# Whole matmuls for the first heads' values, and a last query group in two halves

## The chip, the cores and the metric

The kernel runs on one NeuronCore of a Trainium2 chip. Its engines work side by side and meet only at semaphores: TensorE (PE; its weight loads are the row PEld), VectorE (DVE), ScalarE (ACT), GpSimd (POOL) and SyncE (SP), which issues most DMAs. The metric is device time in microseconds (us) of one execution. The kernel before takes 806.93 us, the median of three executions (806.62, 806.93, 809.84).

## The reference

`x` is 2048 x 640 in bf16. Two attention layers with 32 heads of 20 columns read it, and a gate mixes them:

```python
g = sigmoid((x * gate_w).sum(-1))          # one number per token
qkv = x @ wqkv                             # A and B have weights of their own
# A: every query against all 2048 keys
o_a = softmax(q @ k.T * 20**-0.5) @ v
# B: every query against 8 keys, 0, 2, ... 14 tokens back
o_b = softmax(<q, k[s - 2*w]> * 20**-0.5, w = 0..7) @ v[s - 2*w]
out = g * (o_a @ A_wo) + (1 - g) * (o_b @ B_wo)
```

A is nearly all of the work: 32 x 2048 x 2048 exponentials.

## The kernel before, in words

**Units, tiles and rides.** A's work is cut into 32 groups (`GROUPS`): 512 queries (`qc`, 0 to 3) of four heads (`q`, 0 to 7; `q` 0 holds heads 0 to 3). A group has 64 *units*, one for each of 16 blocks of 128 keys (`kb`) and each of the four heads (`j`). A unit is a 128 x 512 block of scores. `qk` (line 1659) makes two or three units at a time into a PSUM tile `score0` or `score1`, one matmul per unit, the four heads on four 32-row strips of the array. `exp` (L1682) turns the tile into weights in one of five `ebuf` buffers, on ACT. `pv` (L1723) multiplies them with the values `vA` into the PSUM tile `obank`, the heads on four column strips. A unit can instead *ride*: its scores go to a spare bank and DVE makes the exponential with integer arithmetic (L1672, then three shifted copies by L879, each multiplied with values that POOL has scaled into `vS`, L870).

**Order of the work.** `_Sched` records each instruction with a cost in the source. The main loop goes tile by tile: `qk`, `exp`, a `pv` slot, then `spend`, which fills PE with side work (projections, layer B, output products, and filler matmuls of no use to the result, L1744) until a limit after the end of the exponential before. Side work is a set of generators (`gen_...`) with priorities. The table `PLAN` changes the loop's parameters at given tile numbers: the limits (`SLACK`), the conditions for a ride (`DWAIT`, `DIDLE`, `DTIME`, ...), the fillers (`FILL`) and the priorities. Its last entry is for tile 700. All of this runs on the host; what reaches the chip is a fixed list of instructions per engine.

**Start.** The inputs are loaded, `x` is turned on PE, keys and queries of group 0 are made, then `v_first` (L1387 to 1393) makes the values of heads 0 to 3 for key blocks 0 to 3, and `gen_v(0)` (L779) those of blocks 4 to 15 in two banks of six. One block is five accumulating matmuls (the contraction is 640) of 80 columns, and each of these is issued as four matmuls on 32-column strips of the array, with a weight load each: 16 x 5 x 4 = 320 pairs of weight load and matmul. `gen_q1` then makes the queries of group 1.

**Group ends and the kernel's end.** When a group's last `pv` is issued, `close` starts `gen_norm` (L817): DVE transposes `obank` (L819) and takes reciprocals of the sums (L823), POOL (in the last group DVE) scales by them and by the gate (L829, L837), DVE transposes back (L853) and DMAs store the result in `oTd`. For the last group `tail` (L1147) follows: `gen_prefold` has put part of the output product of the last 512 tokens into SBUF (`pre`), `gen_prefold2` another part into two PSUM banks; `tail` adds the rest on PE (L1156), adds up on DVE and ACT (L1173, L1179, L1182) and stores four blocks of 128 tokens (L1187).

Of the kernel before, what the change touches and what calls it, by code (L numbers as in the profile page):

```python
# [14 lines left out]
P = 128  # L15
# [21 lines left out]
VP = lambda q: 0 if q == 0 else 1 if q < 4 else 2  # L37

# [293 lines left out]
def _build(ctx, nc, A_x, A_wqkv, A_wo, B_wqkv, B_wo, gate_w, out):  # L332
# [446 lines left out]
    def gen_v(part):  # L779
        m = (6, 2, 1)[part]  # L780
        for kb in range(4 if part == 0 else 0, KBN, m):
            while part == 2 and g1 < 2 + VPACE * kb / KBN:
                yield ("cond",)
# [610 lines left out]
    def v_out():  # L1394
        return v_copy(0, 0, 4, 0)
# [524 lines left out]
```

## Time and profile before

| | |
|---|---|
| median of three executions | 806.93 us |
| the profiled execution | 807.63 us, its span from first to last instruction 805.8 us |
| mean granted TensorE clock | 0.992 |
| ACT: all busy, and the exponentials alone | 777.7 us, 765.2 us in 727 tiles |
| DVE, PE, POOL busy | 713.9, 759.5, 140.3 us |
| first exponential starts, last exponential ends | 19.35 us, 797.61 us |

Busy time is a share of the span; a busy PE counts matmuls that overlap each other, fillers among them. "issue" in the column of waits is time in which an engine waited for no semaphore that the profile shows. A row of the timeline begins with its start and its length in microseconds.

### The profile page before, as it was taken

The numbers are of one execution on the slowest core, as the hardware profiler recorded it, in microseconds if no ns is written. First come the engines' busy times: TensorE is split into PE (matmuls) and PEld (weight loads), VectorE is DVE, ScalarE is ACT, GpSimd is POOL, SyncE is SP. The second block draws the span as 40 slices with busy tenths as digits, with TensorE's granted clock in tenths as the row PEclk, the third lists the DMA queues.
The fourth block names the chain that finished last, engine by engine and source line by source line (L and its number), as shares of the span: only waits on it lengthen the run. The fifth ranks groups of instructions, "written<-read, shape, count | busy, mean of one in ns | idle before, by whom it ended". The sixth has DMA issues, their size and how long they took to land.

```text
span 805.8 us, 29670 instructions
## 1 busy us (share of the span) xinstructions
PE 759.5 (94%) x12485; PEld 279.4 (35%) x12485; DVE 713.9 (89%) x1286; ACT 777.7 (97%) x762; POOL 140.3 (17%) x239
## 2 busy tenths in 40 slices
PE   8899989999899999999999999899999999999997
PEld 4343232322234333342344344233334333433232
DVE  6568879999989899979889989998998999898995
ACT  4599999999999999999999999999999999999996
POOL 5002411114321111011110111111011111111120
PEclk9799999999999999999999999999999999999999
DMA  9120010112011121031112013003113001303000
GB/s 300 56 46 7 20 28 19 37 32 73 14 26 36 44 55 32 13 78 24 34 48 64 13 39 77 20 21 77 25 32 69 18 23 34 80 7 70 16 7 35
DMA packets 59448, 35.27 MB, mean 44 GB/s; under 512 B 25252, under 2 KB 58116, under 8 KB 59316
## 3 DMA queue, kind: packets, MB, share of 16 engines
q1 hardware_dynamic: 59028, 33.05, 16.6%
q8 instruction: 99, 1.62, 0.8%
q10 hardware_dynamic: 288, 0.33, 0.1%
q14 instruction: 33, 0.27, 0.1%
HBM read 11.45 MB, written 2.62 MB: 17 GB/s over the span
## 4 chain that ended last, share of the span: by engine, by line
ACT 45%; PE 33%; issue 18%; DVE 2%; DMA 1%; SPq 0%; ACTq 0%; DVEq 0%
ACT ebuf L1682 44%; PE score L1659 11%; PE obank L1723 9%; PE side L591 6%; PE score L591 4%; DMA oB<-in_A_x_dram 1%; DVE uD L1672 1%; PE obank L1744 1%; PE side L967 0%; DVE uD L879 0%; PE side L1744 0%; PE score L1334 0%; PE score L1744 0%; ACT eB L998 0%; PE score L967 0%
## 5 line engine op out<-in xcount | busy, mean ns | idle before, releaser
L1682 ACT ACTIVATE ebuf<-score 128x1024 bf16<-128x1024 f32 (+1 forms) x727 | 765.2, 1237 | 11.2 <-PE score L1659 10.4
L1659 PE MATMUL score<-qT,kT 32*128 32x512 bf16 x2023 | 292.4, 385 | 32.0 <-ACT ebuf L1682 23.2
L1672 DVE TENSOR_SCALAR uD<-score 128x512 int16<-128x512 f32 x355 | 237.8, 682 | 17.7 <-PE score L1659 16.5
L879 DVE TENSOR_SCALAR uD<-uD 128x2048 int16<-128x2048 int16 x285 | 192.9, 694 | 10.6 <-PE obank L1723 9.9
L1659 PEld LDWEIGHTS score<-qT,kT 32*128 32x128 bf16 x2023 | 71.3, 91 | 278.5 <-ACT ebuf L1682 211.7
L1723 PE MATMUL obank<-ebuf,vA 128*21 128x512 bf16 x1668 | 165.3, 387 | 0.8 <-DVE uD L879 0.7
L870 POOL TENSOR_TENSOR vS<-vA,vw 128x252 bf16<-128x252 bf16 x95 | 59.9, 632 | 458.0 <-DVE uD L879 238.5
L1723 PE MATMUL obank<-uD,vS 128*21 128x512 bf16 x1140 | 100.4, 379 | 0.0
L591 PE MATMUL side<-xT,kvw 128*32 128x256 bf16 (+1 forms) x2000 | 85.6, 287 | 0.9 <-DVE oB L633 0.5
L1723 PEld LDWEIGHTS obank<-ebuf,vA 128*21 128x21 bf16 x1668 | 40.9, 89 | 99.9 <-issue 77.9
L591 PEld LDWEIGHTS side<-xT,kvw 128*32 128x32 bf16 x2000 | 47.8, 96 | 29.3 <-issue 15.4
L951 DVE TENSOR_TENSOR stage<-qkvB 128x1280 bf16<-128x1280 bf16 x64 | 51.1, 819 | 0.0
L1049 DVE TENSOR_TENSOR stage<-stage,eB 128x1280 bf16<-128x1280 bf16 x64 | 50.9, 821 | 0.0
L837 POOL TENSOR_TENSOR oN<-oTt,rcp 128x256 bf16<-128x256 f32 (+1 forms) x61 | 37.8, 632 | 46.6 <-DVE uD L879 27.2
L591 PE MATMUL score<-xT,kvw 128*32 128x256 bf16 (+2 forms) x760 | 34.8, 291 | 0.3 <-DVE uD L1672 0.3
L1723 PE MATMUL obank<-uD,vA 128*21 128x512 bf16 x380 | 34.3, 379 | 0.0
L935 DVE CAST qkvB<-side 128x512 bf16<-128x512 f32 (+1 forms) x53 | 30.7, 589 | 2.2 <-PE side L591 2.2
L1723 PEld LDWEIGHTS obank<-uD,vS 128*21 128x21 bf16 x1140 | 27.5, 91 | 9.3 <-issue 2.9
L819 DVE STREAM_TRANSPOSE oTt<-obank 128x512 f32<-128x512 f32 x32 | 22.7, 710 | 8.0 <-PE obank L1723 8.0
L591 PE MATMUL side<-kvw,xT 128*32 128x320 bf16 (+2 forms) x680 | 25.7, 283 | 2.1 <-issue 2.1
L829 POOL TENSOR_TENSOR rcp<-rcp,gA 128x16 f32<-128x16 f32 x31 | 6.9, 222 | 115.4 <-DVE rcp L823 40.5
L591 PE MATMUL side<-woBp,oB 128*32 128x128 bf16 (+1 forms) x520 | 24.6, 294 | 0.3 <-DVE oB L1074 0.2
(201 smaller groups left out, 583.1 us busy)
## 6 DMA issues: line engine op xcount, KB each, us to landing
stage<-qkvB SPq DMA_DIRECT2D x128, 82.5 KB
stage<-in_B_wqkv_dram SPq DMA_DIRECT2D x1, 2400.0 KB
oTd<-oN SPq DMA_DIRECT2D x108, 20.0 KB
WqP<-in_A_wqkv_dram SPq DMA_DIRECT2D x13, 160.0 KB
qT<-dst SPq DMA_DIRECT2D x104, 20.0 KB
out_dram<-outsb SPq DMA_DIRECT2D x12, 160.0 KB
kvw<-in_A_wqkv_dram SPq DMA_DIRECT2D x2, 800.0 KB
qT<-qbnd SPq DMA_DIRECT2D x72, 1.0 KB
```

The source lines that it names most:

```text
L591: ins = e.matmul(o[j:k, :], l(j) if callable(l) else l[:, j:k], r, start=(first and i == 0), stop=(last and i == n - 1), skip_group_check= ...
L819: T("dve", 0.623, lambda e: e.transpose(oTt[:, :], obank[:, :]), reads=["obank"], writes=["oTt"])
L837: T(en, c2 if half < 0 else 0.56, lambda e: e.tensor_tensor(oo, ii, ib, ALU.mult), reads=["rcp", "oTt"], writes=[("oN0", h) for h in ((0, ...
L870: T("pool", 0.62, lambda e: e.tensor_tensor(vS[:, d % NVS, :, :], _ap(vA, (kb * NQ + q) * 4 * DV, [[0, K - 1], [1, 4 * DV]]), _ap(vw, 0, [ ...
L879: T("dve", 0.066 + 0.1334 * n, lambda e, k=k: e.tensor_scalar(uD[u][:, 0:512 * n].bitcast(I16), uD[u][:, 0:512 * n].bitcast(I16), SHIFTS[k ...
L935: t = TB(dvc(n * TOK), lambda e, o=o, i=i: e.tensor_copy(o, i), reads=[("side", b)], writes=[key])
L951: TB(dvc(CN * TOK, 2), lambda e, w=w, ks=ks: e.tensor_tensor(prodB(w), qB[:, :, :], ks, ALU.mult), reads=["qB", "kB"], writes=[("prod", w) ...
L1049: TB(dvc(CN * TOK, 2), lambda e, o=o, vs=vs, ee=ee: e.tensor_tensor(o, vs, ee, ALU.mult), reads=["eB", ("prod", k)], writes=[("prod", k + ...
L1659: ins = e.matmul(o, kT[32 * j:32 * j + 32, q, kb * P:(kb + 1) * P], qT[g % NQT][32 * j:32 * j + 32, :], start=True, stop=True)
L1672: t = T("dve", 0.6, lambda e: e.tensor_scalar(uD[d % NU][:, 512 * i:512 * (i + 1)].bitcast(I16), side[y], UOFF, 0.0, op0=ALU.add, op1=ALU. ...
L1682: exps[s] = T("act", actc(512 * n), lambda e: e.activation(ebuf[s % NE][:, 0:512 * n], score[s % 2][:, 0:512 * n], ACTF.Exp, scale=LN2 / S ...
L1723: ins = e.matmul(obank[32 * j:32 * j + DV, :], v, src, start=(kb == 0), stop=(last and k >= len(lst) - 4), skip_group_check=True)
```

## The change

Three things change.

- **Values of heads 0 to 3.** `v_first` makes two key blocks instead of four, `gen_v(0)` the other fourteen in three banks (5, 5 and 4 blocks). Each accumulating step is one matmul over all 128 columns of the array instead of four on strips: 16 x 5 = 80 pairs. Its planned cost is 0.064 us.
- **The last group.** `GROUPS` gets its last entry twice. Both copies are `HALVED`: a unit is still 512 columns wide, but holds 256 queries of *two* key blocks, so each copy has 32 units. `qk` and `pv` issue two matmuls of 256 columns for such a unit; a riding unit needs two scaled sets of values, the second in a part of `xT` that is free by then. Each half has its own `gen_norm` on 256 columns. After the first half `gen_half` finishes and stores token blocks 0 and 1 while the second half runs; `gen_prefold` puts a fourth piece into SBUF, and `tail` is left with blocks 2 and 3.
- **Table.** `PLAN` is replaced as a whole; its last entry is for tile 740. All its parameters are other ones: `SLACK` is mostly (0.28, 0.73) where it was mostly (0.30, 0.64), and up to 0.93 at the end.

The diff, cut to its core:

```diff
+LASTQ = len(GROUPS) - 1
+GROUPS.append(GROUPS[LASTQ])
+HALVED = [False] * LASTQ + [True] * 2
+kbs = lambda g, kb: (2 * kb, 2 * kb + 1) if HALVED[g] else (kb,)
...
 def gen_v(part):
-        m = (6, 2, 1)[part]
-        for kb in range(4 if part == 0 else 0, KBN, m):
+        for kb in (2, 7, 12) if part == 0 else range(0, KBN, m):
...
-                                    mmc(VCN[part]), per=5 if part == 0 else 2 if part == 1 else 1)
+                                    mmc(VCN[part]) if part else 0.064, per=(5, 2, 1)[part], whole=part == 0)
...
 def gen_norm(g):
-        T("dve", 0.623, lambda e: e.transpose(oTt[:, :], obank[:, :]), reads=["obank"], writes=["oTt"])
+        W = 256 if HALVED[g] else 512
+        T("dve", 0.623 if W == 512 else 0.35, lambda e: e.transpose(oTt[:, 0:W], obank[:, 0:W]), reads=["obank"], writes=["oTt"])
...
+    def gen_half():
+        while not (done.get("prefold1") and done.get(("norm", LASTQ))):
+            yield ("cond",)
+        for blk in range(2):
+            b = yield from bank()
+            yield from mm_group(b, fold_mms(side[b][:, :], blk, 0, 512, 1) + fold_mms(side[b][:, :], blk, 0, 512, 2), rd, mmc(512))
+            t = T("dve", dvc(512), lambda e, b=b, blk=blk: e.tensor_tensor(tcol(blk, 0, 512), side[b][:, :], pre(blk), ALU.add), ...)
+        b = yield from bank()
+        for blk in range(2):
+            yield from mm_group(b, fold_mms(o, blk, 512, D, 1) + fold_mms(o, blk, 512, D, 2), rd, mmc(128), per=3)
+        t = T("dve", dvc(256), lambda e, b=b: e.tensor_tensor(trest(0), sap(b, 0, [[P, 2], [1, P]]), prest(0), ALU.add), ...)
+        for blk in range(2):
+            tail_out(blk, "sp")
...
 def tail():
+        T("dve", dvc(256), lambda e: e.tensor_tensor(trest(2), _ap(rest, 0, [[P, 2], [1, P]]), prest(2), ALU.add), ...)
+        T("act", actc(512), lambda e: e.activation(tcol(3, 0, 512), side[tail_bank[3]][:, :], ACTF.Copy), ...)
+        T("dve", dvc(512), lambda e: e.tensor_tensor(tcol(2, 0, 512), side[tail_bank[2]][:, :], pre(3), ALU.add), ...)
+        tail_out(2, "sp")
+        tail_out(3, "act")
...
 def v_first():
-            for kb in range(4):
+            for kb in range(2):
                 for c, (o, l, r) in enumerate(v_mms(side[0][:, 80 * kb:80 * kb + 80], kb, 0)):
-                    for j in range(0, P, 32):
-                        ins = e.matmul(o[j:j + 32, :], l[:, j:j + 32], r, start=(c == 0), stop=(c == CN - 1), skip_group_check=True)
+                    ins = e.matmul(o, l, r, start=(c == 0), stop=(c == CN - 1), skip_group_check=True)
...
 def qk(s):
+            for t in range(2):
+                for g, kb, j, o in lst:
+                    kl = kbs(g, kb)
+                    q, n, c = GROUPS[g][1], 512 // len(kl), 256 * max(0, g - LASTQ)
+                    ins = e.matmul(o[:, n * t:n * t + n], kT[32 * j:32 * j + 32, q, kl[t] * P:(kl[t] + 1) * P],
+                                   qT[min(g, LASTQ) % NQT][32 * j:32 * j + 32, c:c + n], start=True, stop=True)
```

More of the change, by code (lines that the diff above doesn't have):

```diff
@@ L425, in _build @@
     vS = sb([P, NVS, K - 1, 4 * DV], BF16, "vS")
+    vSd = lambda d, t: xT[:, 2 + d % NVS, 0:(K - 1) * 4 * DV].rearrange("p (a b) -> p a b", b=4 * DV) if t else vS[:, d % NVS, :, :]
     gtr0 = qkvB[:, S:S + 1024].bitcast(FP32)
@@ L574, in release, with mm_group @@
         bank_free[b] = t.end + LAT[t.stream]
-    def mm_group(b, mms, reads, cost, first=True, last=True, per=1):
+    def mm_group(b, mms, reads, cost, first=True, last=True, per=1, whole=False):
         n = len(mms)
@@ L588, in fn @@
                     n_ = P if callable(l) else l.shape[-1]
+                    if whole:
+                        ins = e.matmul(o, l, r, start=(first and i == 0), stop=(last and i == n - 1), skip_group_check=True)
+                        continue
                     for j in range(0, n_, 32):
@@ L780, in gen_v @@
         m = (6, 2, 1)[part]
-        for kb in range(4 if part == 0 else 0, KBN, m):
+        for kb in (2, 7, 12) if part == 0 else range(0, KBN, m):
             while part == 2 and g1 < 2 + VPACE * kb / KBN:
                 yield ("cond",)
+            m = 4 if kb == 12 and part == 0 else 5 if part == 0 else m
             b = yield from bank()
@@ L822, in gen_norm @@
         yield ("dve",)
-        T("dve", 0.157, lambda e: e.reciprocal(rcp[:, :], oTt[:, 0:512:32]), reads=["oTt"], writes=["rcp"])
-        en, c1, c2 = ("dve", 0.12, dvc(512)) if g == NG - 1 else ("pool", 0.24, 1.08)
+        T("dve", 0.157 if W == 512 else 0.11, lambda e: e.reciprocal(rcp[:, 0:W // 32], oTt[:, 0:W:32]), reads=["oTt"], writes=["rcp"])
+        en, c1, c2 = ("dve", 0.12, dvc(256)) if g == NG - 1 else ("pool", 0.24, 1.08 if W == 512 else 0.56)
         def scale_o(half):
@@ L832, in emit @@
                         return
-                h0, n = (0, 4) if half < 0 else (2 * half, 2)
+                h0, n = (0, W // 128) if half < 0 else (2 * half, 2)
                 ib = _ap(rcp, 4 * h0, [[4, n], [2, 2], [1, 2], [0, 32]])
@@ L840, in scale_o @@
             return emit
-        if g >= NG - 2:
+        if g >= LASTQ - 1:
             scale_o(-1)(None)
@@ L869, in scale_v @@
         def scale_v(after):
-            T("pool", 0.62, lambda e: e.tensor_tensor(
-                vS[:, d % NVS, :, :], _ap(vA, (kb * NQ + q) * 4 * DV, [[0, K - 1], [1, 4 * DV]]), _ap(vw, 0, [[1, K - 1], [0, 4 * DV]]), ALU.mult),
-              reads=[("vA", kb, VP(q)), "vAones", "vw"], writes=[("vS", d % NVS)], after=after)
+            for t, kk in enumerate(kbs(g, kb)):
+                assert not t or done[("fold", 0, 1)] and done[("gate", QCN - 1)]
+                T("pool", 0.62, lambda e, t=t, kk=kk: e.tensor_tensor(
+                    vSd(d, t), _ap(vA, (kk * NQ + q) * 4 * DV, [[0, K - 1], [1, 4 * DV]]), _ap(vw, 0, [[1, K - 1], [0, 4 * DV]]), ALU.mult),
+                  reads=[("vA", kk, VP(q)), "vAones", "vw"], writes=[("vS2", d % NVS), ("xT", 0, 1)] if t else [("vS", d % NVS)], after=after)
         pool_late.append(scale_v)
@@ L1112, in gen_prefold @@
             yield ("cond",)
-        for i in range(3):
+        for i in range(4):
             while i == 2 and not done.get(("b", 2 * QCN - 1)):
                 yield ("cond",)
-            rd = OT(0) + [("oB", hu, f0) for hu in range(1 + (i == 2)) for f0 in range(0, CN, 2)]
+            rd = OT(0) + [("oB", hu, f0) for hu in range(1 + (i >= 2)) for f0 in range(0, CN, 2)]
             b = yield from bank()
-            if i < 2:
-                yield from mm_group(b, fold_mms(side[b][:, :], i, 0, 512, 0), rd, mmc(512))
+            if i != 2:
+                yield from mm_group(b, fold_mms(side[b][:, :], (0, 1, 2, 2)[i], 0, 512, 0), rd, mmc(512))
             else:
@@ L1124, in gen_prefold @@
             t = T("dve", dvc(512), lambda e, b=b, i=i: e.tensor_copy(pre(i), side[b][:, :]), reads=[("side", b)],
-                  writes=[("pre", i)] + [[("dst", 0), ("dst", 1)], [("qabs", 0), ("qabs", 1)], [("prod", w) for w in range(5)]][i])
+                  writes=[("pre", i)] + [[("dst", 0), ("dst", 1)], [("qabs", 0), ("qabs", 1)], [("prod", w) for w in range(5)], [("prod", w) for w in range(5, WIN)]][i])
             release(b, t)
@@ L1138, in gen_prefold2 @@
     def gen_prefold2():
-        while not (done.get("prefold1") and d_over() and done.get(("norm", NG - 2))):
+        while not (done.get("prefold1") and d_over() and done.get(("norm", LASTQ - 1))):
             yield ("cond",)
         rd = OT(0) + [("oB", hu, f0) for hu in range(2) for f0 in range(0, CN, 2)]
-        for blk in (2, 3):
+        for blk in (3, 2):
+            while blk == 2 and not done.get("first half"):
+                yield ("cond",)
             b = yield from bank()
-            yield from mm_group(b, fold_mms(side[b][:, :], blk, 0, 512, 0), rd, mmc(512), last=False)
-            yield from mm_group(b, fold_mms(side[b][:, :], blk, 0, 512, 1), OT(1), mmc(512), first=False, last=False)
+            if blk == 3:
+                yield from mm_group(b, fold_mms(side[b][:, :], blk, 0, 512, 0), rd, mmc(512), last=False)
+            yield from mm_group(b, fold_mms(side[b][:, :], blk, 0, 512, 1), OT(1), mmc(512), first=blk == 2, last=False)
@@ L1146, in gen_prefold2, with tail_out @@
             tail_bank[blk] = b
         done["prefold"] = True
+    tout = [_ap(stage, 3 * 1024 + blk * D, [[1, D]]) for blk in range(4)]
+    tcol = lambda blk, c0, c1: _ap(stage, 3 * 1024 + blk * D + c0, [[1, c1 - c0]])
+    trest = lambda blk: _ap(stage, 3 * 1024 + 512 + blk * D, [[D, 2], [1, P]])
+    prest = lambda blk: stage[:, 2048 + 256 * blk:2048 + 256 * (blk + 2)].bitcast(FP32).rearrange("p (b c) -> p b c", c=P)
+    def tail_out(blk, eng):
+        row = (QCN - 1) * 512 + blk * P
+        T(eng, 2.0, lambda e: e.dma_start(out_v[row:row + P, :], tout[blk]),
+          reads=[("tout", blk), ("tout_r", blk // 2)], writes=[("out", row)], dma=True)
@@ new lines, in gen_half @@
+    def gen_half():
+        while not (done.get("prefold1") and done.get(("norm", LASTQ))):
+            yield ("cond",)
+        rd = OT(1) + ["oN1"] + WL
+        for blk in range(2):
+            b = yield from bank()
+            yield from mm_group(b, fold_mms(side[b][:, :], blk, 0, 512, 1) + fold_mms(side[b][:, :], blk, 0, 512, 2), rd, mmc(512))
+            yield ("dve",)
+            t = T("dve", dvc(512), lambda e, b=b, blk=blk: e.tensor_tensor(tcol(blk, 0, 512), side[b][:, :], pre(blk), ALU.add),
+                  reads=[("side", b), ("pre", blk), ("pre", 2)], writes=[("tout", blk)])
+            release(b, t)
+        b = yield from bank()
+        for blk in range(2):
+            o = side[b][:, blk * P:(blk + 1) * P]
+            yield from mm_group(b, fold_mms(o, blk, 512, D, 1) + fold_mms(o, blk, 512, D, 2), rd, mmc(128), per=3)
+        yield ("dve",)
+        t = T("dve", dvc(256), lambda e, b=b: e.tensor_tensor(trest(0), sap(b, 0, [[P, 2], [1, P]]), prest(0), ALU.add),
+              reads=[("side", b), ("pre", 2)], writes=[("tout_r", 0)])
+        release(b, t)
+        for blk in range(2):
+            tail_out(blk, "sp")
+        done["first half"] = True
@@ L1149, in tail, with mm @@
     def tail():
-        tout = [_ap(stage, 3 * 1024 + blk * D, [[1, D]]) for blk in range(4)]
-        tcol = lambda blk, c0, c1: _ap(stage, 3 * 1024 + blk * D + c0, [[1, c1 - c0]])
-        def mm(key, lst, accum, rd=["oN1"] + WL, per=1, last=True):
+        def mm(key, lst, accum, rd=["oN1"] + WL, per=1, last=True, cost=0.215):
             def fn(e):
@@ L1157, in fn @@
                 return ins
-            T("pe", sum(0.215 if o.shape[-1] > 128 else 0.06 for o, _, _ in lst), fn, reads=rd, mode="col",
+            T("pe", cost * len(lst), fn, reads=rd, mode="col",
               **({"accum": [key]} if accum else {"writes": [key]}))
-        b3 = score[1]
-        late = [("score", 0), [(score[0][:, blk * 512:(blk + 1) * 512], blk, 0, 512) for blk in range(2)]], [
-            ("score", 1), [(b3[:, blk * P:(blk + 1) * P], blk, 512, D) for blk in range(4)]]
+        rest = score[1]
+        outs = [(rest[:, (blk - 2) * P:(blk - 1) * P], blk, 512, D) for blk in (2, 3)]
         for k in range(2):
-            for key, outs in late[::1 - 2 * k]:
-                mm(key, [fold_mms(*a, 1)[k] for a in outs], k > 0, OT(1), 1 if len(outs) == 2 else 4, False)
-        mm(("score", 1), [fold_mms(*a, 2)[0] for a in late[1][1]], True)
+            mm(("score", 1), [fold_mms(*a, 1)[k] for a in outs], k > 0, OT(1), 2, False, 0.06)
+        mm(("score", 1), [fold_mms(*a, 2)[0] for a in outs], True, cost=0.06)
         for blk in (2, 3):
@@ L1171, in tail @@
             mm(("side", b), fold_mms(side[b][:, :], blk, 0, 512, 2), True)
-        mm(("score", 0), [fold_mms(*a, 2)[0] for a in late[0][1]], True)
-        T("dve", dvc(512), lambda e: e.tensor_tensor(
-            _ap(stage, 3 * 1024 + 512, [[D, 4], [1, P]]), _ap(b3, 0, [[P, 4], [1, P]]),
-            stage[:, 2048:3072].bitcast(FP32).rearrange("p (b c) -> p b c", c=P), ALU.add),
-          reads=[("score", 1), ("pre", 2)], writes=["tout_r"])
-        for blk in (2, 3):
-            b = tail_bank[blk]
-            T("act", actc(512), lambda e, b=b, blk=blk: e.activation(tcol(blk, 0, 512), side[b][:, :], ACTF.Copy),
-              reads=[("side", b)], writes=[("tout", blk)])
-        for blk in range(2):
-            T("dve", dvc(512), lambda e, blk=blk: e.tensor_tensor(
-                tcol(blk, 0, 512), score[0][:, blk * 512:(blk + 1) * 512], pre(blk), ALU.add),
-              reads=[("score", 0), ("pre", blk)], writes=[("tout", blk)])
-        for blk in (2, 3, 0, 1):
-            row = (QCN - 1) * 512 + blk * P
-            T("act" if blk > 1 else "sp", 2.0, lambda e, blk=blk, row=row: e.dma_start(out_v[row:row + P, :], tout[blk]),
-              reads=[("tout", blk), "tout_r"], writes=[("out", row)], dma=True)
+        T("dve", dvc(256), lambda e: e.tensor_tensor(trest(2), _ap(rest, 0, [[P, 2], [1, P]]), prest(2), ALU.add),
+          reads=[("score", 1), ("pre", 2)], writes=[("tout_r", 1)])
+        T("act", actc(512), lambda e: e.activation(tcol(3, 0, 512), side[tail_bank[3]][:, :], ACTF.Copy),
+          reads=[("side", tail_bank[3])], writes=[("tout", 3)])
+        T("dve", dvc(512), lambda e: e.tensor_tensor(tcol(2, 0, 512), side[tail_bank[2]][:, :], pre(3), ALU.add),
+          reads=[("side", tail_bank[2]), ("pre", 3)], writes=[("tout", 2)])
+        tail_out(2, "sp")
+        tail_out(3, "act")
     def gen_fold(qc, hu):
@@ L1478, in _build @@
     add_gen(gen_qd(), QPRIO)
-    NG = QCN * NQ
-    ahead = [[0, KBN] for g in range(NG)]
+    NG = len(GROUPS)
+    ahead = [[0, KBN // 2 if h_ else KBN] for h_ in HALVED]
     tiles = []
@@ L1487, in _build @@
     pvq = []
-    left_a = [KBN * 4] * NG
+    left_a = [KBN * (2 if h_ else 4) for h_ in HALVED]
     left_d = [0] * NG
@@ L1656, in fn @@
             ins = None
-            for g, kb, j, o in lst:
-                q = GROUPS[g][1]
-                ins = e.matmul(o, kT[32 * j:32 * j + 32, q, kb * P:(kb + 1) * P], qT[g % NQT][32 * j:32 * j + 32, :],
-                               start=True, stop=True)
+            for t in range(2):
+                for g, kb, j, o in lst:
+                    kl = kbs(g, kb)
+                    if t == len(kl):
+                        continue
+                    q, n, c = GROUPS[g][1], 512 // len(kl), 256 * max(0, g - LASTQ)
+                    ins = e.matmul(o[:, n * t:n * t + n], kT[32 * j:32 * j + 32, q, kl[t] * P:(kl[t] + 1) * P],
+                                   qT[min(g, LASTQ) % NQT][32 * j:32 * j + 32, c:c + n], start=True, stop=True)
             return ins
@@ L1686, in exp, with vs_keys @@
             bank_free[x] = exps[s].end + LAT["act"]
+    def vs_keys(d):
+        return [("vS2" if t else "vS", d % NVS) for t in range(2 if HALVED[dquads[d][0]] else 1)]
     def slice_keys(d):
@@ L1694, in pv, with add @@
         rd = set()
+        def add(g, kb, j, v, src, i):
+            kl = kbs(g, kb)
+            n = 512 // len(kl)
+            k = len(lst) // (4 * len(kl))
+            for t, kk in enumerate(kl):
+                lst.append((k, t, g, kk, j, v(t, kk, j), src[:, 512 * i + n * t:512 * i + n * t + n]))
         for uu in units:
@@ L1705, in pv @@
             if k:
[L1706 removed]
+                rd.update(vs_keys(d))
             done[("pk", d, k)] = True
             for i, j in enumerate(ridden[d]):
[L1709 to L1710 removed]
+                add(g, kb, j, lambda t, kk, j, d=d, k=k, g=g: vSd(d, t)[:, k - 1, j * DV:(j + 1) * DV] if k else vA[:, kk, GROUPS[g][1], j, :],
+                    uD[d % NU], i)
             left_d[g] -= len(ridden[d])
+        lst = [x[2:] for x in sorted(lst, key=lambda x: x[:2])]
         for g, kb, j, _, _ in lst:
@@ L1722, in fn @@
             for k, (g, kb, j, v, src) in enumerate(lst):
-                ins = e.matmul(obank[32 * j:32 * j + DV, :], v, src,
+                ins = e.matmul(obank[32 * j:32 * j + DV, 0:src.shape[-1]], v, src,
                                start=(kb == 0), stop=(last and k >= len(lst) - 4), skip_group_check=True)
             return ins
-        T("pe", 0.2195 * ((len(lst) + 3) // 4), fn, reads=sorted(rd, key=str), accum=["obank"], mode="col")
+        T("pe", (0.11 if HALVED[g] else 0.2195) * ((len(lst) + 3) // 4), fn, reads=sorted(rd, key=str), accum=["obank"], mode="col")
         return last
@@ L1808, in pv_slot @@
                 run_until(("ds", d, k), DHIGH)
-            elif not end_g and sch.ready(*slice_keys(d), *([("vS", d % NVS)] if k else [])) > sch.avail["pe"]:
+            elif not end_g and sch.ready(*slice_keys(d), *(vs_keys(d) if k else [])) > sch.avail["pe"]:
                 continue
@@ L1828, in slices_ready @@
         return sum(1 for d in range(cur["pv"], len(dquads)) if dquads[d][0] == pvg and closed[d] and kq[d] < K and done.get(
-            ("ds", d, kq[d])) and sch.ready(*slice_keys(d), *([("vS", d % NVS)] if kq[d] else [])) <= sch.avail["pe"])
+            ("ds", d, kq[d])) and sch.ready(*slice_keys(d), *(vs_keys(d) if kq[d] else [])) <= sch.avail["pe"])
     s = 0
```

27 lines of the change are left out of this document (14 added, 13 removed), and 123 rows, old and new, of the table PLAN.

## The prediction

> **What bounds the kernel now.** I read the page's busy times first, then the groups by shape, then who waited for whom on ACT, and then the timeline of the two places where ACT is not busy.
>
> ```profile
> PE 759.5 (94%) x12485; PEld 279.4 (35%) x12485; DVE 713.9 (89%) x1286; ACT 777.7 (97%) x762; POOL 140.3 (17%) x239
> ...
> q8 instruction: 99, 1.62, 0.8%
> ```
>
> ```profile
> L1682 ACT ACTIVATE ebuf<-score 128x1024 bf16<-128x1024 f32 x511 | 498.2, 1109 | 2.4 <-PE score L1659 1.7
> L1682 ACT ACTIVATE ebuf<-score 128x1536 bf16<-128x1536 f32 x215 | 312.2, 1544 | 8.8 <-PE score L1659 8.7
> ```
>
> ```profile
> ACT ebuf L1682 <- PE score L1659: 10.4, 8, 6.5
> ```
>
> ACT is the bound, and nearly all of its time is exponentials: 511 x 2 + 215 x 3 + 1 = 1668 units of 2048, the other 380 ride on DVE. Tiles of two and three units differ by 1544 - 1109 = 435 ns, so a unit costs ACT 0.435 us. Of the 10.4 us that ACT waited for scores, 6.5 are one wait. The timeline of the start shows it (ACT, then PE):
>
> ```profile
> 19.35 1.45 ACT L1682 ACTIVATE ebuf<-score 128x1536 bf16<-128x1536 f32 x1 [0.65 <-PE score L1659]
> 27.31 2.36 ACT L1682 ACTIVATE ebuf<-score 128x1536 bf16<-128x1536 f32 x2 [6.51 <-PE score L1659]
> 31.19 1.45 ACT L1682 ACTIVATE ebuf<-score 128x1536 bf16<-128x1536 f32 x1 [1.52 <-PE score L1659]
> ...
> 19.23 0.32 PE L591 MATMUL score<-kvw,xT 128*32 128x80 bf16 x13
> 21.26 1.85 PE L591 MATMUL score<-kvw,xT 128*32 128x80 bf16 x107 [1.71 <-issue]
> 22.85 0.60 PE L591 MATMUL side<-kvw,xT 128*32 128x80 bf16 x21
> 25.53 1.19 PE L591 MATMUL side<-kvw,xT 128*32 128x80 bf16 x59 [2.08 <-issue]
> 26.66 1.03 PE L1659 MATMUL score<-qT,kT 32*128 32x512 bf16 x5
> ```
>
> The scores of the second tile (26.66) stand in PE's queue behind 200 small matmuls for the values of heads 0 to 3, and PE twice stops among them for 1.71 and 2.08 us with no semaphore to wait for ("issue"). Between the stops lie 107 + 21 = 128 matmuls, with their weight loads 256 instructions. The page's queue q8 moved 99 instruction packets, and PE has 2 x 12485 = 24970 recorded instructions: 252 per packet. So a packet is about 256 PE instructions, and PE stops when a packet is used up before the next has come: the DMA view has one q8 packet between 18 and 20 us, one between 22 and 24.5 and one between 26 and 28, about one in 4 us. Seventeen nanoseconds a pair (1.85 us over 107) use up a packet in 2.2 us. The granted clock falls after the first stop, and the next scores and the projection behind them run at half rate, which makes the 1.52 us wait at 31.19 (stretch, its length, busy time of PE, PEld, DVE, ACT and POOL, granted clock, DMA share, GB/s):
>
> ```profile
> 20.00:24.00 4.00, 2.19 (x128) 2.01 (x128) 2.61 (x6) 0.80 (x1) 1.42 (x2) 0.68 0.61 242
> 24.00:28.00 4.00, 2.47 (x90) 1.51 (x94) 0.54 (x2) 0.69 (x1) 0.00 (x0) 0.50 0.02 6
> ```
>
> The other place is the end. The last exponential ends at 797.61 and the run at 805.8, 8.2 us of one chain, on DVE mostly:
>
> ```profile
> 798.11 0.72 DVE L819 STREAM_TRANSPOSE oTt<-obank 128x512 f32<-128x512 f32 x1 [3.64 <-PE obank L1723]
> ...
> 799.36 0.75 DVE L837 TENSOR_TENSOR oN<-oTt,rcp 128x512 bf16<-128x512 f32 x1
> 800.14 0.45 DVE L853 STREAM_TRANSPOSE oN<-oN 128x256 f32<-128x256 f32 x1
> 801.10 0.69 DVE L1173 TENSOR_TENSOR stage<-score,stage 128x512 bf16<-128x512 f32 x1 [0.52 <-PE score L1156]
> 801.96 0.69 DVE L1182 TENSOR_TENSOR stage<-score,dst 128x512 bf16<-128x512 f32 x1 [0.17 <-PE score L1156]
> 802.57 0.68 DVE L1182 TENSOR_TENSOR stage<-score,qabs 128x512 bf16<-128x512 f32 x1
> ```
>
> **The values of the first heads.** 320 pairs become 80, so 480 instructions go, nearly two packets of 256. The work itself stays: the strips took 0.90 us for 80 and 17 ns each behind, 0.90 + 240 x 0.017 = 5.0 us in all; the nearest row for a whole matmul is the turning of x (128 columns on 128), 20 in 1.29 us by the chain of waits, 65 ns, and 80 x 65 ns = 5.2 us. But a packet then lasts 128 x 65 ns = 8.3 us, twice the 4 us that one takes to come, so neither stop is left. The first stop lies 13 pairs into the second run of values. With the change 10 pairs stand in for the 80 of `v_first`, so behind the first tile's scores 70 + 13 = 83 pairs are left in the packet, more than the 70 of `gen_v(0)`: the packet that came at 21.26 is wanted only about 19.2 + 70 x 0.065 = 24 us.
>
> What then holds the second tile is the planner's limit: the end of the first exponential (20.80) plus 0.64 us, entry 0 of the table before and after. PE stops side work there, the scores start about 21.3, and ACT follows 0.44 us after the start of its scores (18.91 to 19.35). So the second exponential starts about 21.7 and the wait is 0.9 us instead of 6.51: **-5.6 us**. The clock has no reason to fall, since PE stays busy, so the wait at 31.19 shrinks too; I leave it 0.3 of its 1.52: **-1.2 us**. Ends for the two together: at the least the two stops alone, -3.8; at the most both waits in full, -8.0. I take -6.8, nearer the upper end, because the limit leaves 0.9. DVE, which copies the values out, had 0.54 us of work between 24 and 28 us, so an earlier start finds it free. Later transfers lose 7 us of slack; nothing in the waits of ACT between 32 and 797 us is a DMA.
>
> The Trainium skill, "TensorEngine Tiling (Array Packing)", section "Key Properties", says that changing the tiling mode drains TensorE, which speaks against whole matmuls among strips. In the trace three score matmuls on row strips are followed 0.32 us later by column strips (18.91, 19.23), about 0.1 us more than the 0.21 us that four more strips cost elsewhere (x4 in 0.39, x8 in 0.60 us); with two more changes for each of 14 blocks on the path the sum would be 2.8 us higher.
>
> **The last group.** In the chain after the last exponential widths halve. The rows of half the width: DVE on 256 f32 columns 0.42 us (L1074), the transpose of 256 0.44 (L853), DVE on 128 columns 0.28 (L737). So `pv` -0.1, first transpose 0.72 to 0.44, scaling 0.75 to 0.42, second transpose 0.45 to 0.28: -0.88. The additions at the end, 801.10 to 803.25 = 2.15 us, become one of 256 and one of 512, 0.42 + 0.69 plus a gap of 0.1: -0.94. The store behind them (SP, 2.5 us from 803.25 to the end) stays, with one issue less before it. Together **-1.8 us**; ends -0.9 (if the last store is held by something else) and -2.6 (if the reciprocal and the gaps shrink as well).
>
> What it adds runs beside ACT: the first half's norm, three additions (0.69, 0.69, 0.42) and one more copy to SBUF (0.68) on DVE, about 4 us, the two stores on SP, and the second scaled set on POOL (0.63 us a quad, POOL is 17% busy). The cover is this:
>
> ```profile
> 790.00:797.00 7.00, 7.00 (x99) 2.08 (x95) 2.79 (x4) 7.00 (x7) 0.36 (x1) 1.00 0.02 5
> ```
>
> DVE has 4.2 us free there, about as much as is wanted; without that cover 0.7 us per operation would delay the second half's norm, at most 2 us. The 64 units of halves issue twice the matmuls with the same columns, about 19 instructions a microsecond for scores and products, against 60 (a packet of 256 in 4 us) that can be brought. The second half's `pv` must wait for the first half's transpose, as at every group's end (8.0 us of DVE waits for `obank` over 9 ends, none of ACT).
>
> **The table.** It changes every tile, and no row prices it. What it can move is the number of rides and the number of tiles. Ten units more on DVE are -4.4 us of ACT, and 10 x (0.68 + 3 x 0.69 / 4) = 12 us of DVE, which has 761 - 689 = 72 us free between 36 and 797 us; ten fewer are +4.4. If all entries up to 740 are reached there are at least 14 tiles more, each costing between 0 and 3 x 1109 - 2 x 1544 = 239 ns: 0 to +3.3. I take 0, between the two signs, and keep -5 and +6 for the range.
>
> **Sum.** The profiled execution took 807.63 us (span 805.8 and 1.8 around it): 807.6 - 6.8 - 1.8 = 799.0. It stood 0.7 above the median of 806.93, so against that the forecast is **798.3 us**. Half a per cent, 4 us, is about what can be told from no change here: faster means under 802.9, slower over 811.0.
>
> **Rivals.**
>
> *More rides.* The table also moves ten units or more to DVE: 794 us and below. For it: DVE's 72 us free. Against: DVE is full where B's work lies (9.97 of 10 us at 750 to 760).
>
> *The gain is eaten further on.* Only the two stops go (-3.8), the tail gives 0.9 and tiles cost 1: 807.6 - 3.7 - 0.7 = 803.2. For it: the start's 7 us of delay also gave loads and projections time.
>
> *Late scores (slower).* Scores start 0.44 us before their exponential, and side work may run 0.73 us, at the end 0.93, past the end of the exponential before, where it was 0.64. A tile of three keeps ACT busy for 312.2 / 215 = 1.45 us, so 1.45 - 0.44 - 0.73 = 0.28 us stay for PE's lateness where there were 0.37. If PE runs later than its planned costs by more than that, ACT waits at every tile. It decides from 8.6 + 4 = 12.6 us over 727 tiles, 17 ns each; at 25 ns the time is 798.3 + 18 = 816 us. Against: ACT's whole wait in the middle, 36 to 797, is 2.4 us today.
>
> *The fetch does not matter.* If instruction supply is hidden and the 6.5 us come from loads that end at 22 us, only the tail remains: 805.1. That is what the Trainium skill says, "Runtime: NRT & Kernel Launch", section "Instruction fetch mechanics": fetch in blocks of 256 instructions is hidden by issue. The block size agrees with 252 per packet here; the hiding doesn't, with two stops of 1.71 and 2.08 us 128 pairs apart.
>
> **Chances.** Forecast case 0.55, more rides 0.22, eaten 0.09, late scores 0.11, fetch 0.03. Faster: 0.55 + 0.22 = 0.77; same 0.12; slower 0.11. The range leaves out late scores and a little below: 791 (798.3 less 5 for the table and 2 for the ends) to 805. The forecast case alone is 795 to 802.
>
> **What would show it.** Second exponential at about 21.7 us; no "issue" stop in L591 before 30 us; clock 1.00 in 20 to 32; last exponential to end about 6.4 us; 370 to 390 rides. Wrong if ACT's waits for scores grow beyond 5 us in the middle, or if rides fall by 20.

## The result, and the profile after

The changed kernel takes 802.56 us (median of 20 executions, 801.93 to 808.41) against 806.45 us (20 executions, 805.13 to 809.89): a ratio of 0.9956 with a 95% interval of 0.9942 to 0.9970. It is 3.9 us faster, less than half of the 8.6 us that the forecast gave. The profiled execution took 802.58 us with a span of 800.7 us (807.63 and 805.8 before).

The page's busy times, then the exponentials by shape and the rides on DVE:

```profile
PE 769.5 (96%) x12489; PEld 283.7 (35%) x12489; DVE 713.5 (89%) x1286; ACT 780.5 (97%) x777; POOL 145.1 (18%) x243
```

```profile
L1731 ACT ACTIVATE ebuf<-score 128x1024 bf16<-128x1024 f32 x555 | 533.1, 1084 | 1.4 <-PE score L1708 0.7
...
L1731 ACT ACTIVATE ebuf<-score 128x1536 bf16<-128x1536 f32 x187 | 270.3, 1507 | 1.4 <-PE score L1708 1.1
L1721 DVE TENSOR_SCALAR uD<-score 128x512 int16<-128x512 f32 x313 | 209.0, 680 | 25.5 <-PE score L1708 24.7
...
L1721 DVE TENSOR_SCALAR uD<-side 128x512 int16<-128x512 f32 x63 | 42.8, 679 | 2.5 <-PE side L1708 2.4
```

313 + 63 = 376 units ride where 380 did, so ACT makes four units more, and it makes them in 743 tiles instead of 727. What ACT waits for scores fell from 10.4 us to 1.7:

```profile
ACT ebuf L1731 <- PE score L1708: 1.7, 6, 0.5
```

The start in the timeline, ACT first. For 21 us from the first exponential on, ACT is not idle:

```profile
19.14 21.43 ACT L1731 ACTIVATE ebuf<-score 128x1536 bf16<-128x1536 f32 x20 [0.49 <-PE score L1708]
```

PE's rows show whole matmuls (128*128) and no "issue", and the second tile's scores (20.02) come after 25 of them:

```profile
19.02 1.07 PE L602 MATMUL score<-kvw,xT 128*128 128x80 bf16 x25
20.02 0.39 PE L1708 MATMUL score<-qT,kT 32*128 32x512 bf16 x2
20.64 0.39 PE L1708 MATMUL score<-qT,kT 32*128 32x512 bf16 x3 [0.23 <-ACT ebuf L1731]
20.96 0.89 PE L602 MATMUL side<-kvw,xT 128*128 128x80 bf16 x20
```

The stretches that had a granted clock of 0.68 and 0.50 before have 1.00 now (columns as in the prediction):

```profile
20.00:24.00 4.00, 3.66 (x56) 1.96 (x53) 3.83 (x10) 4.00 (x5) 1.37 (x2) 1.00 0.60 240
24.00:28.00 4.00, 3.68 (x55) 1.39 (x56) 2.32 (x17) 4.00 (x4) 0.61 (x1) 1.00 0.02 6
```

The end. The last exponential ends at 792.4 us, the run at 800.7: 8.3 us, as long as before. DVE's chain is shorter, and then DVE waits 2.07 us for PE:

```profile
793.14 0.45 DVE L840 STREAM_TRANSPOSE oTt<-obank 128x256 f32<-128x256 f32 x1
...
794.06 0.46 DVE L858 TENSOR_TENSOR oN<-oTt,rcp 128x256 bf16<-128x256 f32 x1
794.56 0.31 DVE L874 STREAM_TRANSPOSE oN<-oN 128x128 f32<-128x128 f32 x1
796.93 0.42 DVE L1227 TENSOR_TENSOR stage<-score,stage 128x256 bf16<-128x256 f32 x1 [2.07 <-PE score L1213]
797.28 0.68 DVE L1231 TENSOR_TENSOR stage<-score,stage 128x512 bf16<-128x512 f32 x1
```

The chain of waits names what PE did: 40 + 8 matmuls of `gen_prefold2` (L606), which the host's list had put behind the last product of the group and ahead of the tail's own (L1213).

```profile
792.57 0.52 PE obank L1783 x16
793.08 0.01 issue
793.10 2.45 PE side L606 x40
795.55 0.66 PE score L606 x8
796.21 0.89 PE score L1213 x28
```

An account of the two profiled executions, from the starts of the exponentials in the trace. Where ACT is not held up, the next exponential starts 0.904 us after one of two units and 1.330 us after one of three (medians). So the tiles alone need 511 x 0.904 + 215 x 1.330 + 0.48 = 748.4 us before and 555 x 0.904 + 187 x 1.330 + 0.48 = 750.9 us after; the rest between first and last exponential is delay.

| us | before | after | difference |
|---|---|---|---|
| first exponential starts | 19.35 | 19.14 | -0.2 |
| delay of ACT up to 36 us | 8.5 | 0.1 | -8.5 |
| tiles alone | 748.4 | 750.9 | +2.5 |
| delay of ACT behind 36 us | 21.2 | 22.2 | +1.0 |
| last exponential's end to the run's end | 8.2 | 8.3 | +0.1 |
| span | 805.8 | 800.7 | -5.1 |

(The columns hold the median steps; the last step of an exponential is its full length.) The profiled execution before lay 1.2 us above its median, the one after on it, so that the medians differ by 3.9.

### The profile page after: what moved, and what is told of

It is laid out like the page before. It is cut to its first block, busy times and chain, and to the rows that moved or that the text cites. A ratio compares the mean times of both kernels' runs of the same rounds, so it can differ in the third digit from the quotient of the medians.

```text
span 800.7 us, 29678 instructions
## 1 busy us (share of the span) xinstructions
PE 769.5 (96%) x12489; PEld 283.7 (35%) x12489; DVE 713.5 (89%) x1286; ACT 780.5 (97%) x777; POOL 145.1 (18%) x243
## 4 chain that ended last, share of the span: by engine, by line
ACT 41%; PE 38%; issue 15%; DVE 4%; DMA 1%; SPq 0%; ACTq 0%
ACT ebuf L1731 40%; PE score L1708 13%; PE obank L1783 10%; PE side L606 7%; PE score L606 6%; DVE uD L1721 2%; DVE uD L902 1%; DMA oB<-in_A_x_dram 1%; PE score L990 0%; DVE kmd L651 0%; DVE qkvB L648 0%; ACT eB L1021 0%; PE score L1380 0%; PE obank L1804 0%; PE side L1804 0%
## 5 line engine op out<-in xcount | busy, mean ns | idle before, releaser
L1708 PE MATMUL score<-qT,kT 32*128 32x512 bf16 (+1 forms) x2044 | 297.9, 378 | 22.8 <-ACT ebuf L1731 15.7
L1721 DVE TENSOR_SCALAR uD<-score 128x512 int16<-128x512 f32 x313 | 209.0, 680 | 25.5 <-PE score L1708 24.7
L1783 PE MATMUL obank<-ebuf,vA 128*21 128x512 bf16 (+1 forms) x1724 | 165.4, 380 | 0.6 <-DVE uD L902 0.4
L1783 PE MATMUL obank<-uD,vS 128*21 128x512 bf16 (+1 forms) x1128 | 98.2, 376 | 0.0
L606 PE MATMUL side<-xT,kvw 128*32 128x256 bf16 (+1 forms) x1960 | 82.6, 285 | 0.4 <-DVE uD L1721 0.3
L606 PEld LDWEIGHTS side<-xT,kvw 128*32 128x32 bf16 x1960 | 47.1, 96 | 26.4 <-issue 12.5
L1721 DVE TENSOR_SCALAR uD<-side 128x512 int16<-128x512 f32 x63 | 42.8, 679 | 2.5 <-PE side L1708 2.4
L606 PE MATMUL score<-xT,kvw 128*32 128x256 bf16 (+2 forms) x800 | 39.9, 296 | 0.7 <-ACT ebuf L1731 0.7
L1783 PE MATMUL obank<-uD,vA 128*21 128x512 bf16 (+1 forms) x388 | 33.6, 372 | 0.0
L1783 PEld LDWEIGHTS obank<-uD,vS 128*21 128x21 bf16 x1128 | 26.8, 91 | 11.5 <-issue 4.8
L850 POOL TENSOR_TENSOR rcp<-rcp,gA 128x16 f32<-128x16 f32 (+1 forms) x32 | 7.8, 245 | 111.3 <-DVE rcp L844 49.5
L840 DVE STREAM_TRANSPOSE oTt<-obank 128x512 f32<-128x512 f32 (+1 forms) x33 | 22.8, 691 | 3.6 <-PE obank L1783 3.4
L1708 PE MATMUL side<-qT,kT 32*128 32x512 bf16 (+1 forms) x68 | 24.2, 366 | 0.0
```

The lines of the kernel that those rows point to most:

```text
L606: ins = e.matmul(o[j:k, :], l(j) if callable(l) else l[:, j:k], r, start=(first and i == 0), stop=(last and i == n - 1), skip_group_check= ...
L840: T("dve", 0.623 if W == 512 else 0.35, lambda e: e.transpose(oTt[:, 0:W], obank[:, 0:W]), reads=["obank"], writes=["oTt"])
L1708: ins = e.matmul(o[:, n * t:n * t + n], kT[32 * j:32 * j + 32, q, kl[t] * P:(kl[t] + 1) * P], qT[min(g, LASTQ) % NQT][32 * j:32 * j + 32, ...
L1721: t = T("dve", 0.6, lambda e: e.tensor_scalar(uD[d % NU][:, 512 * i:512 * (i + 1)].bitcast(I16), side[y], UOFF, 0.0, op0=ALU.add, op1=ALU. ...
L1783: ins = e.matmul(obank[32 * j:32 * j + DV, 0:src.shape[-1]], v, src, start=(kb == 0), stop=(last and k >= len(lst) - 4), skip_group_check= ...
```

## The experiments

The theory after the result: PE ran out of instruction packets at the start, and that is gone; the halves save DVE time at the end, but PE has become the end's bound. The rivals: the new order and table made the start fast, not the count of instructions; and the end is DVE's chain or the stores. The kernel before took 806.92 us beside e1 to e4 and 807.10 beside e5 to e8, so times of different sets can be compared to no better than about half a microsecond.

**Strips again, nothing else (e1).** The plan on the host stays the same to the last instruction's place; only the instructions of the values differ.

```diff
-                        ins = e.matmul(o, l, r, start=(first and i == 0), ...)
+                        for j in range(0, P, 32):
+                            ins = e.matmul(o[j:j + 32, :], l[:, j:j + 32], r, start=(first and i == 0), ...)
```

> The changed kernel with one thing undone: each of the 80 whole matmuls for the values of heads 0 to 3 is issued as four matmuls on 32-column strips again, at the same planned cost, so that order and table stay. Theory (PE runs out of instruction packets at the start): the two stops come back between 19 and 27 us, the second exponential starts after 25 us instead of 20.5, and the time rises by 6 to 9 us over the changed kernel's 802.6, to 809 to 811. Rival (the new order and table made the start fast, not the count of instructions): within 1 us of 802.6.

806.35 us, ratio to the kernel before 0.9992 (0.9981 to 1.0003): 4 us above the changed kernel, half of what was expected, and the second exponential started at 22.25 us, not after 25. The stops are back (timeline, PE):

```profile
18.90 0.68 PE L603 MATMUL score<-kvw,xT 128*32 128x80 bf16 x53
21.28 0.61 PE L603 MATMUL score<-kvw,xT 128*32 128x80 bf16 x47 [1.71 <-issue]
21.82 0.60 PE L1710 MATMUL score<-qT,kT 32*128 32x512 bf16 x5
22.36 0.86 PE L603 MATMUL side<-kvw,xT 128*32 128x80 bf16 x76
25.02 0.22 PE L603 MATMUL side<-kvw,xT 128*32 128x80 bf16 x4 [1.80 <-issue]
```

Here 40 pairs precede the first scores instead of 80, and the first stop comes after 53 pairs instead of 13: 40 later. The second comes 47 + 5 + 76 = 128 pairs behind the first, as before. Counted from the start of the trace, both kernels stop at the same places: behind 220 recorded matmuls and 220 weight loads, and again behind 348 of each. So the stops stand at places in the count of instructions, 256 apart; they go with no buffer or semaphore. The size was off because the order matters too: the changed kernel asks for the second tile's scores after 5 blocks instead of 10, so they wait for the first stop alone. ACT's delay up to 36 us is 4.0 us here, 8.5 before, 0.1 in the changed kernel. The granted clock falls here too, but later and for a shorter time: it is 1.00 from 20 to 24 us and 0.51 from 26.5 to 30 (before: 0.50 from 24 to 28, 0.54 from 28 to 32).

**Whole matmuls in the kernel before, nothing else (e2).**

```diff
 def v_first():
-                    for j in range(0, P, 32):
-                        ins = e.matmul(o[j:j + 32, :], l[:, j:j + 32], r, ...)
+                    ins = e.matmul(o, l, r, ...)
 def gen_v(part):
-                                    mmc(VCN[part]), per=...)
+                                    mmc(VCN[part]), per=..., whole=part == 0)
```

> The kernel before with only the 320 strip matmuls of the first heads' values issued as 80 whole ones; planned costs, order, table and end stay. Theory (instruction packets): no stop of PE between 19 and 27 us, 50 whole matmuls of some 0.04 us before the second tile's scores instead of 200 small ones and two stops, the second exponential at about 21.9 us (27.3 before), the clock stays at 1.0, and the time falls by 6.5 to 8.5 us to 798 to 800. Rival (order and loads hold the second tile): above 804.

801.61 us, ratio 0.9939 (0.9925 to 0.9953): this one edit gives 5.3 us. The whole change gave 3.9, and 4.8 when it ran again (e6, below). The intervals of the ratios overlap, so the edit gives as much as the whole change; that it gives more is not shown. The delay up to 36 us fell from 8.5 to 2.1 us, the clock stays at 1.00. The time is 1.6 us above the expectation, and the trace has a wait of 1.1 us that the expectation did not have: the second tile's scores go to a bank that still holds values, and DVE's copy of them stood behind three instructions on a constant (PE, then DVE):

```profile
22.50 0.60 PE L1661 MATMUL score<-qT,kT 32*128 32x512 bf16 x5 [1.14 <-DVE vA L776]
```

```profile
19.84 0.96 DVE L517 TENSOR_SCALAR KMd<-outsb 128x160 bf16<-128x160 f32 x1
20.84 1.03 DVE L519 SCALAR_TENSOR_TENSOR KMd<-outsb,KMd 128x160 bf16<-128x160 f32 x1
21.79 0.65 DVE L776 CAST vA<-score 128x480 bf16<-128x480 f32 x1
```

**The same with these copies first (e8).** The finished list of DVE instructions is changed by one move: the three on the constant go behind the third copy of values (`late_dve` and `v_copies` hold places noted while the list was made).

```diff
+    dl = sch.lists["dve"]
+    moved = dl[late_dve[0]:late_dve[0] + 3]
+    dl[late_dve[0]:late_dve[0] + 3] = []
+    at = dl.index(v_copies[2]) + 1
+    dl[at:at] = moved
     sch.emit()
```

> The kernel before with whole matmuls for the first heads' values, and with three DVE instructions on a constant (2.2 us at 19.6 to 21.9 in the run without this) moved behind the copies of these values. There the second tile's scores waited 1.14 us for a copy that stood behind them. Theory (that copy was the last thing that held the second tile): the second exponential starts at 21.8 to 22.2 instead of 22.9 us, the time falls by about 1 us to 800 to 801. Rival (PE's 50 matmuls hold it anyway): 801.3 to 802.

801.17 us, ratio 0.9921 (0.9904 to 0.9939), the fastest of the kernels whose work is complete: 5.9 us below the kernel before. The changed kernel ran once more beside it (e6), so that the two can be compared on one chip:

> The changed kernel as it is, beside the others on the same chip: 802 to 803.5.

802.28 us, ratio 0.9938 (0.9921 to 0.9954). The 1.1 us between them, and the 0.6 us that e8 gains over e2, are within the intervals, and e8's time lies between its two expectations. The trace decides: the step from the first exponential to the second fell from 3.43 us (19.50 to 22.93) in e2 to 2.32 (19.09 to 21.41), so the copy did hold the second tile; 0.88 us are still PE's matmuls:

```profile
21.41 9.14 ACT L1687 ACTIVATE ebuf<-score 128x1536 bf16<-128x1536 f32 x8 [0.88 <-PE score L1664]
```

**Less side work at the end (e3).** The changed kernel without the first part of block 3's product in `gen_prefold2`, 32 of its matmuls; the result of this block is not complete.

```diff
-            if blk == 3:
-                yield from mm_group(b, fold_mms(side[b][:, :], blk, 0, 512, 0), rd, mmc(512), last=False)
-            yield from mm_group(b, fold_mms(side[b][:, :], blk, 0, 512, 1), OT(1), mmc(512), first=blk == 2, last=False)
+            yield from mm_group(b, fold_mms(side[b][:, :], blk, 0, 512, 1), OT(1), mmc(512), first=True, last=False)
```

> The changed kernel without the 32 matmuls that add the first part of the output product for token block 3 at the end (that block's output lacks layer B and part of A). Theory (PE is the end's bound: 48 matmuls of side work stand in its queue behind the last product and ahead of the tail's): the tail's matmuls start about 1.3 us earlier, where DVE's chain then holds them, and the time falls by 1.0 to 1.9 us to 800.7 to 801.6. Rival (DVE's chain or the last stores set the end): 802.3 to 802.8.

800.66 us, 0.9924 (0.9911 to 0.9937): 1.9 us below the changed kernel's 802.56, which comes from another set of runs. In the traces last exponential to end is 798.4 - 791.7 = 6.7 us instead of 8.3; what else the spans differ by is mostly an earlier first exponential (18.55 us instead of 19.14). The forecast of 6.4 was for an end that PE does not hold. PE's list is what held it: DVE's wait for the tail's matmuls fell from 2.07 us to 0.40.

**The halves in the kernel before (e4), and with whole matmuls (e5).** Both have the old table, banks and planned costs, and everything of the changed kernel that concerns the last group; e5 has the two edits of e2 on top.

```diff
+GROUPS.append(GROUPS[LASTQ])
+HALVED = [False] * LASTQ + [True] * 2
 (and with them gen_norm, gen_d, gen_prefold, gen_prefold2, gen_half, tail, qk and pv of the changed kernel)
```

> The kernel before with only the last group in two halves; table and values of the first heads as before. Theory (the halves put more work on PE ahead of the end than ACT's last exponentials cover): last exponential to end stays at 8 us or more, and the time is 806 to 808. Rival (the new table alone spoiled the end): last exponential to end 6.4 us, time 804.5 to 805.

> The kernel before with whole matmuls for the first heads' values and with the last group in halves, but with its own table, banks and planned costs. Theory (the parts add up: whole matmuls -5.3, halves +4.6 as measured alone): 805.5 to 807, so that the table and the new order of the values are worth 3 to 4 us in the changed kernel. Rival (the halves lose only because of the slow start): 800 to 802.

e4 takes 811.54 us, ratio 1.0061 (1.0043 to 1.0078): 4.6 us slower, more than expected. e5 takes 806.35 us, 0.9998 (0.9983 to 1.0013), as the parts add up. In both the end is 3 us longer: 809.8 - 798.5 = 11.3 us and 805.4 - 793.9 = 11.5 us. The chain of e4 shows that 36 of the 48 matmuls of `gen_half`, and 8 of `gen_prefold2`, stood behind the last product:

```profile
798.54 0.86 PE obank L1776 x24
...
801.19 3.62 PE score L599 x40
804.81 1.43 PE score L1205 x27
```

There they also wait for the second half's norm (PE idles 1.82 us until DVE's transpose, L866, ends at 801.1), and the granted clock is 0.54 from 801 to 807 us in e4 and 0.50 from 797 to 803 in e5. The tail's own 32 matmuls take 1.9 us there, and 1.2 in the changed kernel at a clock of 1.00. The 3 us are the price of queue, wait and clock together; they were not taken apart. Why this list had no room for `gen_half` earlier was not tested either; the old table's limits are the likely reason. The list of e4 and e5 has a fault as well: the second half's norm writes the same 256 columns of `oN` as the first's, so the matmuls behind it use the second half's values for blocks 0 and 1. The work has the same size, but it is not the time of a plan that is right.

The other 1.5 us or so of e4: four units more on ACT (376 rides) are 1.7 us of tiles alone (750.1 against 748.4).

**The last group whole, with the new table (e7).** The changed kernel with all that concerns the last group as in the kernel before.

```diff
-GROUPS.append(GROUPS[LASTQ])
-HALVED = [False] * LASTQ + [True] * 2
 (and with them gen_norm, gen_d, gen_prefold, gen_prefold2, tail, qk and pv of the kernel before; no gen_half)
```

> The changed kernel with its table and its values of the first heads, but with the last group whole and the end of the kernel before. Theory (PE's queue eats what the halves save at the end): within 1.2 us of the changed kernel, last exponential to end 8 to 9.3 us. Rival (the forecast's 1.8 us are there after all and something else was lost): 1.8 us or more above the changed kernel.

803.73 us, 0.9956 (0.9939 to 0.9973): 1.45 us above the changed kernel's 802.28 (every execution lies above all of that kernel's in this set), between the two expectations, and its end is 801.8 - 792.0 = 9.8 us, longer than the 8 to 9.3 of the theory. With the new table the halves do gain 1.5 us; but a whole last group has a worse end with the new table than with the old one, 9.8 against 8.2. Its chain again has side work of PE behind the last product:

```profile
792.05 0.40 PE obank L1733 x4
792.44 0.33 PE side L601 x4
792.77 2.38 PE score L601 x40
795.15 1.87 PE score L1167 x63
```

A reason may be layer B: its last output is written to `oB` at 770.2 us before, 776.3 in the changed kernel and 780.0 here, and the pieces that need it come no earlier. That was not tried by itself, because each change of priorities makes another list of instructions for all that follows.

What table and halves are worth depends on each other. Without the halves, the new table with the new order of the values costs about 2 us (801.61 in e2, 803.73 here). With the halves, as e4 and e5 have them, it gives 4.1 (806.35 in e5, 802.28 in e6).

## Why the prediction was right or wrong

The sign, the place and the range were right, the size was not: 8.6 us forecast, 3.9 measured, and 802.56 us lies just outside the 795 to 802 of the forecast case. The steps that failed are the last group and the table. They stood in the sum with -1.8 and 0. Together they came to +3.6 in the traces: +2.5 of tiles, +1.0 of waits behind 36 us, +0.1 at the end, which PE held and not DVE.

- **The start** held, and gave more than its term: -8.5 us of ACT's delay for -6.8, past the end of -8.0, since the planner let the second exponential start without the 0.9 us that I had left (it takes the scores after 25 matmuls, well inside the limit). Instruction packets as the cause: shown by e1, where the stop moves by the 40 pairs that were taken away, and by e2. The Trainium skill, "Runtime: NRT & Kernel Launch", section "Instruction fetch mechanics", has the fetch hidden by issue; with its block of 256 instructions the runs agree, with the hiding they don't (stops of 1.71 and 1.80 us in e1, and 4 us of time). But "fetch" and "order" are not two terms that add: the count alone takes 6.4 us off the delay (e2), the order alone 4.5 (e1 against before), both 8.5.
- **The whole matmul** was priced at 65 ns by the turning of x. It took (1.07 - 0.20) / 24 = 36 ns, where 0.20 us is the mean length of one. It changed nothing: at 36 ns a packet of 128 pairs still lasts 4.6 us, longer than the 4 us that one takes to come. The 17 ns a strip were misread: over the row's 1.85 us the granted clock is 0.55 on average. At 1.00 the 80 pairs of `v_first` took 0.90 us, so strips use up a packet sooner than the 2.2 us of the prediction. The drain that the Trainium skill names for a change of tiling mode ("TensorEngine Tiling (Array Packing)", section "Key Properties"), +2.8 us by my bound, cost ACT nothing that the trace shows: its delay there is 0.1 us.
- **The last group**, -1.8 us, failed by its cover. Its DVE terms were right: from the first transpose to the second's end 2.48 us became 1.73, and the additions take 1.03 instead of 2.15. But the cover was read for DVE only. The row that I showed for 790 to 797 us has PE busy for 7.00 of 7.00 us, none of it with fillers, and the halves put product, norm and stores of blocks 0 and 1 into that stretch. What did not fit went behind the last product, where it delays the tail: +0.1 us at the end for -1.8 as a whole, +3.0 with the old table and its list (e4), -1.5 only against the longer end that the new table makes by itself (e7). e3 shows 1.6 us at the end that 32 of these matmuls cost.
- **The table**, taken as 0 between -5 and +6, is the larger miss. Four rides fewer (4 x 0.426 = 1.7 us) and 16 tiles more (16 x 0.052 = 0.8, as 3 x 0.904 - 2 x 1.330 = 0.052) cost +2.5 us, also without the halves (e7), the waits behind 36 us +1.0 (+0.4 in e7), and the end of a whole group 9.8 instead of 8.2, +1.6. Together that is +5.1, inside its range; with the -1.5 of the halves and the -8.7 of the start it makes the 5.1 us by which the spans differ. This split takes the table first. With the halves first (e4, e5) the loss falls on them instead, and only the sum of the two, +3.6, does not depend on the order. The 14 tiles that were read off the table's last entry were there (16); "ten rides more or less" was four.
- **Late scores**, the slower rival, did not come: 22.2 us of delay behind 36 us against 21.2. "The gain is eaten further on" (803.2) named the right time, but only half of the reason, so its time is partly luck: the start came in full, the eating was at the end and in the tiles.

## What to carry to other kernels

Count the instructions, not only the time, where an engine does many small matmuls early: here, where PE waited for them, 256 came about every 4 us, and 80 whole matmuls did the work of 320 with a quarter of the fetch. An edit that is "hidden beside other work" needs a cover on every engine that it uses; the row that shows one engine's free time shows the full one beside it. Before a compound change is kept, run its parts alone: here one part alone gave 5.3 us, as much as the whole, and what the others gave or cost depended on what stood with them.

## What the runs showed of the hardware

A whole matmul of 128 x 128 weights and 80 columns, weight load included, follows the one before it after 36 ns (25 in 1.07 us) at a granted clock of 1.00. Four strips of 32 columns take 4 x 9 ns at that clock (80 in 0.90 us, less 0.20 for the last one's length) and nearly twice as much where the clock was 0.55 on average (107 in 1.85 us). Strips were no faster even without a stop.

PE's stop is not over when its packet has landed. In the trace before, the packets' transfers began at 18.87 and 22.93 us and took 1.10 and 1.02 us, and PE went on at 21.26 and 25.53: 1.3 and 1.6 us later. No other packet came in between.

When a packet is asked for can be read where PE does not wait. In the changed kernel PE is at its 440th and 696th recorded instruction at 24.41 and 34.26 us, the places of the two stops of the kernel before, and packets begin at 24.64 and 34.71 us. So the packet of a block begins to come about when PE enters the block before it. PE could go on 4.27 us after it had entered a block in the kernel before (21.26 to 25.53) and 3.74 us in e1 (21.28 to 25.02), so a block that is used up sooner ends in a stop. PE's 184th instruction, 256 ahead of the first stop, ran at 13.1 us in the kernel before, but the next packet began only at 18.87, while the loads of the start had the DMA engines full (share 1.07 from 13 to 18.8 us). So these loads may well have a part in the first stop; no run takes them away. They have little in the second: the share was 0.14 from 22.9 to 23.9 us, when its packet came.
